# Earlier copies of second products, half of the taps' copies on VectorE, and an earlier last maximum, in a one-core convolution and mixture kernel

## The chip, the core and the metric

The kernel runs on one core of a Trainium2 chip. Its engines are TensorE (PE in the profile, its weight loads PEld), VectorE (DVE), ScalarE (ACT), GpSimd (POOL) and SyncE (SP), which only issues DMAs here. Each engine takes its own instructions in the order in which they are written, and waits for the others by semaphores. The metric is the device time of one execution in microseconds, the median of several runs; lower is better.

## The reference

The input is 8 sequences of 4160 positions with 192 numbers each. A causal convolution with 7 taps, softmax weights and 8 heads of 24 columns comes first; each of the 33280 rows then passes a layer with 1024 hidden columns:

```python
w = softmax(weight)                       # 8 heads x 7 taps
x = sum_k w[head, k] * x_pad[s + k]       # causal, per head
h = x @ w_in                              # 192 -> 1024
e = np.exp(h - h.max(-1))
solu = h * e / (e.sum(-1) + 1e-09)
ln = (solu - mean(solu)) / np.sqrt(var(solu) + 1e-06) * g_ln
out = ln @ w_out                          # 1024 -> 192
```

## The kernel before

The 33280 rows are 260 tiles of 128 rows. A tile i passes these stages, each a function that emits one or a few instructions:

- first products `ph` (PE): 128x1024 sums in one of three pairs of PSUM banks, from `yT` (the convolved rows, transposed) and the halves `whi`, `wlo` of `w_in`. The "thirds" are products of 64 rows each (line 794) that close a sum or open it.
- `emit_max` (DVE, L867): scales `ph` in place and finds the row's extreme. `emit_exp` (ACT, L874): exponentials `e` with their sum. `emit_mul` (DVE, L884): `e` times `ph`; it is the last reader of `ph`, so the pair of banks is free after it.
- `emit_hi` (ACT, L895, for some early tiles POOL, L893) and `emit_lo` (POOL, L910): the two halves `p` of `e` in 16 bits, and a transposing DMA `pT<-p`. `emit_square` (ACT, L899): sum of squares.
- `emit_out` (PE, L945, in the middle of the run L812): the second product `po` from `pT` and the halves `ohl` of `w_out`, some six tiles later, into one of two single PSUM banks. `emit_evac` (DVE, L986): the copy of `po` into `raw`, which frees that bank. Rows are scaled and stored later.

The two single banks are handed out in turn by `single`; other users of them are the convolution's products `pc` (L299) and, in four places, the taps. So a second product must wait for the copy of the second product before it whenever one other user stands between them.

The order on every engine is that of the emitting code. `three_steps(i)` emits three tiles a, b, c = i, i+1, i+2 and the second products of three earlier ones (`done`), for i = 8, 11, ... 29 and for i = 254; `two_steps` emits two tiles for 32 to 253; `leave_two` finishes the last pair; `last_three(257)` ends the program. Below, "step 17" is `three_steps(17)`, and "maximum of 17" is `emit_max` of tile 17.

`split_taps(q)` prepares the convolution's taps in 16 bits for the chunks from the fourth on. It runs four times: once at the last place of step 14 and at three places of step 17 (ahead of the first copy, inside `second()`, and ahead of the maximum of c). Each takes a single bank, `tph`, writes 448 columns with two matmuls (L611), and copies the high and low halves out on ACT (L617), 128x224 each.

In step 17 and step 20, `second()` (the second product of `done[1]` and the place of work after it) and the copy of `done[1]` stand after the multiplication of a. In `two_steps` the maximum of b is the last DVE work of the pair but one; the two copies of its pair of second products come at the start of the next pass or of `leave_two`.

Of the kernel before, what the change touches and what calls it, by code (L numbers as in the profile page):

```python
# [20 lines left out]
def kernel(  # L21
# [21 lines left out]
    NT = B * S // P  # L43
# [32 lines left out]
    act, dve, pool = nc.scalar, nc.vector, nc.gpsimd  # L76
# [499 lines left out]
    taps_hi = cp.tile([P, H, CW], F16, name="taps_hi")  # L576
# [5 lines left out]
    def of_blocks(t, a, z):  # L582
        return t[:, :, a * TB : z * TB].rearrange("p h (q c) -> p q h c", c=TB)
# [23 lines left out]
    def split_taps(q):  # L607

        t = single(f"tph_{q}")
        for j in range(2):  # L610
            nc.tensor.matmul(  # L611
                t[:, 2 * j * H * TB : 2 * (j + 1) * H * TB], spread(q + j),
                b16.rearrange("p a h c -> p (a h c)"), start=j == 0, stop=j == 1,
            )
        got = t[:, 0 : 4 * H * TB].rearrange("p (q a h c) -> p a q h c", q=2, a=2, h=H)
        for j, to in enumerate((taps_hi, taps_lo)):
            act.copy(of_blocks(to, q, q + 2), got[:, j])  # L617


    t_in = cp.tile([P, 1], F32, name="t_in")  # L620
# [243 lines left out]
    def emit_max(t):  # L864

        t.bias = sp.tile([P, 1], F32, name=f"sm_{t.i}", tag="sm", bufs=4)
        dve.tensor_scalar(  # L867
            t.ph, t.ph, t.cv[:, 0:1], None, ALU.mult, ALU.min, accum_out=t.bias
        )
# [12 lines left out]
    def emit_mul(t):  # L882

        dve.scalar_tensor_tensor(  # L884
            t.e, t.ph, t.cv[:, 3:4], t.e, ALU.mult, ALU.mult,
            accum_out=t.grp.s1[:, t.g : t.g + 1],
        )
# [92 lines left out]
    def emit_evac(t):  # L980
        if t.grp.raw is None:
            t.grp.open()
        if not t.wide:
            dve.tensor_copy(t.grp.raw[:, t.g, :], t.po[:, 0:D])
        else:
            dve.tensor_reduce(  # L986
                t.grp.raw[:, t.g, :],
                t.po[:, 0 : 2 * D].rearrange("p (a d) -> p d a", a=2), AX.X, ALU.add,
            )
        (rows if t.grp.ready else t.grp.waiting).append((t.grp, t.g))  # L990
# [432 lines left out]
    def three_steps(i):  # L1423
# [43 lines left out]
        def second():  # L1467
            for d in done[1:2]:
                emit_out(d)
            place(2)  # L1470
# [88 lines left out]
        if start:  # L1559
            if not behind:  # L1560
                root_squares()
            second()
            if i > PAIRED:
                if not behind:
                    for k, h in late:
                        sum_up(k, h, i - 1)
                    late.clear()
                uppers(2)
            for k, q in doubles:
                k.double(*q)  # L1570
            doubles.clear()
        emit_mul(a)
        if i == PAIRED:
            uppers(2)
# [17 lines left out]
        if start:  # L1592
            loads(work)
        else:
            second()
            uppers(2)
        for d in done[1:2]:
            emit_evac(d)
        run_chain(4)
        queue.run(3.8 if i < 20 else 2.0)  # L1600
        if start:
# [107 lines left out]
    def two_steps(i):  # L1709


        a, b = prepare(i), prepare(i + 1)
        x, z = tiles[i - 6], tiles[i - 5]
        ch, s = b.ch, b.k // 2
        c1, c3 = (chunks[ch + j] if ch + j < NCH else None for j in (1, 3))

        run_stores()
        first = ch == 3
        when = (2, 3, 5, 6) if first else (0, 1, 2, 4)
        if c3 and s in when:  # L1720
            c3.load(when.index(s))
        evacs = []
        if left_over:
            pa, pb, *evacs = left_over
            emit_exp(pb)
        else:
            pa = pb = None
        for d in evacs:
            emit_evac(d)
        if pb:  # L1730
            emit_mul(pb)

        got, summed = [], False
        sa, sb, sc = ring
        up_half(a, sa, 0)
        up_half(b, sb, 0)
        up_half(a, sa, 1)
        if s % 2 and c1:
            j = s - 1
            got, half, bank = fold(c1, c1.groups()[j : j + 2], sc)  # L1740
            out_half(x, z, 0, slice(0, 6))
            half(0)
            out_half(x, z, 0, slice(6, NFC))
            half(1)
            if chain and chain[0][1] is not None and chain[0][1] <= i + 2:
                add_up(i + 2, bank)
                summed = True
            ring[:] = [sa, sc, sb]
        else:
            out_half(x, z, 0)  # L1750
            ring[:] = [sc, sa, sb]
        up_half(b, sb, 1)
        out_half(x, z, 1)

        def move():
            for f in moves[:1]:
                f()
            del moves[:1]

        if pa:  # L1760
            emit_square(pa)
            emit_hi(pb)
            emit_lo(pa, pool)
        else:
            for q in squares:
                emit_square(q)
            squares.clear()
        for k, q in doubles:
            k.double(*q)
        doubles.clear()  # L1770
        move()
        emit_max(a)
        emit_exp(a)
        queue.run(1.3)
        for _ in range(2 + (len(rows) > 8)):
            if rows:
                g, j = rows.pop(0)
                g.row(j, act if j % 2 else dve)
        if not summed:
            run_chain(3)  # L1780
        if c3:
            for j in (
                ((), (), (), (0, 1), (2,), (3,), (4, 5), (6, 7)) if first
                else ((), (0,), (1,), (2,), (3,), (4,), (5, 6), (7,), ())
            )[s]:
                sum_up(c3, c3.halves(j // 2)[j % 2], i)
        for k, pc, hg in got[:1]:
            k.upper(pc, *hg)
        emit_mul(a)
        for k, pc, hg in got[1:]:  # L1790
            k.upper(pc, *hg)
        for k, pc, hg in got:
            k.lower(pc, *hg)
        if pb:
            emit_square(pb)
            emit_lo(pb, pool)
            queue.run(1.3)
        move()
        emit_hi(a)
        if summed:  # L1800
            run_chain(1)
        emit_max(b)
        run_chain(4)
        queue.run(1.3)
        if got and s in (3, 7):
            part = c1.parts[s == 7]
            if s == 3:
                c1.open(lefts[c1.ch], chunks[ch])
            moves.extend(
                lambda blk=blk: c1.turn(blk, *part) for blk in (1, 0, 2)  # L1810
            )
            moves.append(lambda: doubles.append((c1, part)))
        take_rooted()
        left_over[:] = [a, b, x, z]

    def leave_two():

        a, b, *done = left_over
        run_stores()
        emit_exp(b)  # L1820
        for d in done:
            emit_evac(d)
        emit_mul(b)
        emit_square(a)
        emit_hi(b)
        emit_lo(a, pool)
        emit_lo(b, pool)
        squares.append(b)

    def last_three(i):  # L1830


        a, b, c = [prepare(i + j) for j in range(3)]
        done = tiles[i - DEPTH : i]
        assert all(t.grp.n == 1 for t in (*done[4:], a, b, c))
        run_stores()
        take_rooted()
        emit_out(done[0])
        done = done[1:]
        emit_a(a, b, c, lambda: emit_out(done[0]), slots=tuple(ring))  # L1840
        for t in (b, c):
            emit_rows(t, False, True)
        for t in squares:
            emit_square(t)
        emit_evac(tiles[i - DEPTH])
        emit_evac(done[0])
        emit_max(a)
        emit_exp(a)
        emit_max(b)
        emit_exp(b)  # L1850
        emit_out(done[1])
        emit_mul(a)
        emit_halves(a, pool)
        emit_mul(b)
        emit_max(c)
        emit_out(done[2])
        emit_halves(b, pool)
        emit_exp(c)
        emit_evac(done[1])
        emit_evac(done[2])  # L1860
        emit_out(done[3])
        emit_mul(c)
        ready(done[4])
        emit_finish(done[3])
        emit_halves(c, dve)
        for t in (a, b, c):
            emit_square(t)
        emit_out(done[4])
        emit_finish(done[4])
        take_rooted()  # L1870
        queue.run(100.0)
        emit_out(a)
        ready(a)
        emit_finish(a)
        ready(b)
        ready(c)
        while rows or rooted:
            take_rooted()
            run_rows(i)
        run_stores()  # L1880
        for t in (b, c):
            emit_out(t)
            emit_finish(t)
        assert not stores and not queue.items
# [38 lines left out]
```

## Time and profile before

| | us |
|---|---|
| median of 3 runs (lowest, highest) | 1140.63 (1140.18, 1142.14) |
| profiled execution, its own time | 1142.65 |
| span in its profile | 1140.9 |
| PE busy | 1118.9 |
| ACT busy | 996.2 |
| DVE busy | 989.8 |
| POOL busy | 893.0 |

The span runs from the first to the last instruction; what lies around it (1.75 us) belongs to the execution's own time. Rows of a timeline give start, duration, engine, line, operation, output and inputs, partitions x elements, and in brackets how long the engine sat idle just before and who released it. The granted TensorE clock is 1.00 over the whole run.

### The profile page before, as it was taken

The page shows a single profiled execution, that of the slowest core. Times are in us where ns is not written, and L with a number is a line of the kernel's source. Part 1 is how long each engine was busy: PE and PEld are TensorE (multiplying, and loading weights), DVE is VectorE, ACT ScalarE, POOL GpSimd, SP SyncE. Part 2 cuts the span into 40 slices and gives each one's busy share as a digit, 9 for nine tenths or more (in the row PEclk, how much of TensorE's full clock was granted, in tenths as well). Part 3 has the DMA queues.
Part 4 walks back from the last instruction along what each step waited for, and adds up shares of the span by engine and source line. Part 5 has one row for each costly group of instructions (what it writes and reads, how often), then busy time and mean ns, then how long its engine had stood idle before and what let it go on. Part 6 is the DMA issues. An engine that isn't in the chain of part 4 may idle for free.

```text
span 1140.9 us, 34827 instructions
## 1 busy us (share of the span) xinstructions
PE 1118.9 (98%) x13693; PEld 912.7 (80%) x13693; DVE 989.8 (87%) x2024; ACT 996.2 (87%) x1789; POOL 893.0 (78%) x711
## 2 busy tenths in 40 slices
PE   6999999999999999999999999999999999999998
PEld 3675658878889988888888988888898888887866
DVE  7988898888898888889889888888988888878787
ACT  7888998888889888888888888898888889888895
POOL 2866899968889697888868879698787969855664
PEclk9999999999999999999999999999999999999999
DMA  7998999999999999999999999999999988779977
GB/s 220 197 188 181 218 216 195 198 216 213 225 211 204 225 190 207 206 200 208 208 191 202 195 212 218 178 208 209 210 212 204 216 185 156 183 155 212 184 151 180
DMA packets 727473, 227.75 MB, mean 200 GB/s; under 512 B 651646, under 2 KB 725902, under 8 KB 727310
## 3 DMA queue, kind: packets, MB, share of 16 engines
q1 hardware_dynamic: 727310, 225.53, 99.8%
q8 instruction: 108, 1.77, 0.7%
q14 instruction: 55, 0.45, 0.1%
HBM read 33.00 MB, written 25.56 MB: 51 GB/s over the span
## 4 chain that ended last, share of the span: by engine, by line
PE 70%; issue 9%; DVE 9%; ACT 6%; POOL 3%; DMA 2%; SPq 1%; DVEq 0%; ACTq 0%; POOLq 0%
PE ph L812 30%; PE po L812 28%; DVE ph L867 5%; PE pc L812 5%; PE po L945 3%; PE ph L765 2%; ACT e L874 2%; POOL p L910 2%; DVE e L884 1%; ACT sq L899 1%; DVE y L340 1%; PE pc L299 1%; DMA pT<-p 1%; DMA raw_in<-in_moe_w_in_dram 1%; PE ph L794 1%
## 5 line engine op out<-in xcount | busy, mean ns | idle before, releaser
L910 POOL TENSOR_TENSOR p<-e,p 128x1024 f16<-128x1024 f32 x257 | 548.5, 2137 | 113.0 <-ACT p L895 111.9
L812 PE MATMUL po<-ohl,pT 64*128 64x192 f16 (+1 forms) x5952 | 500.3, 283 | 1.2 <-DMA pT<-p 1.2
L812 PE MATMUL ph<-whi,yT 64*128 64x512 f16 x2664 | 487.6, 376 | 0.0
L812 PEld LDWEIGHTS <-pT 64*128 64x128 f16 x5952 | 401.5, 94 | 36.6 <-issue 4.2
L884 DVE SCALAR_TENSOR_TENSOR e<-ph,cv,e 128x1024 f32<-128x1024 f32 x248 | 318.0, 1283 | 115.4 <-ACT e L874 114.1
L812 PEld LDWEIGHTS <-yT 64*128 64x128 f16 x3774 | 288.6, 94 | 89.6 <-DMA yT<-y 0.5
L874 ACT ACTIVATE e<-ph,sm 128x1024 f32<-128x1024 f32 x260 | 289.6, 1114 | 78.2 <-DVE ph L867 67.2
L867 DVE TENSOR_SCALAR_CACHE_REDUCE ph<-ph,cv 128x1024 f32<-128x1024 f32 x248 | 318.7, 1287 | 1.8 <-PE ph L794 0.7
L812 PE MATMUL ph<-wlo,yT 64*128 64x512 f16 x1110 | 294.8, 376 | 0.0
L895 ACT CAST p<-e 128x1024 f16<-128x1024 f32 x245 | 255.8, 1045 | 41.8 <-DVE e L884 39.8
L899 ACT ACTIVATE sq<-e 128x1024 f32<-128x1024 f32 x260 | 273.3, 1051 | 0.2
L812 PE MATMUL po<-ohl,sixth 64*128 64x384 f16 (+1 forms) x1152 | 155.5, 283 | 0.0
L986 DVE TENSOR_REDUCE raw<-po 128x192 f32<-128x384 f32 x247 | 126.7, 550 | 1.8 <-PE po L945 1.7
L261 POOL TENSOR_TENSOR xs<-xr,xs 128x960 f16<-128x960 f32 (+1 forms) x56 | 107.7, 1924 | 0.8
L812 PEld LDWEIGHTS <-sixth 64*128 64x128 f16 x1152 | 102.6, 94 | 7.0 <-DMA sixth<-p 0.4
L812 PE MATMUL ph<-wlo,y 64*128 64x512 f16 x222 | 83.5, 376 | 0.3 <-DMA y<-yT 0.2
L945 PE MATMUL po<-ohl,pT 128*128 128x192 f16 (+1 forms) x696 | 78.2, 268 | 3.0 <-DVE raw L986 1.9
L945 PEld LDWEIGHTS <-pT 128*128 128x128 f16 x696 | 60.5, 98 | 21.7 <-issue 5.3
L812 PE MATMUL pc<-xs,taps_hi 64*112 64x240 f16 (+1 forms) x832 | 77.1, 258 | 0.2
L183 DVE TENSOR_REDUCE xa<-xr 128x1 f32<-128x384 f32 x112 | 67.6, 619 | 1.6 <-DMA xr<-in_x_dram 1.6
L340 DVE SCALAR_TENSOR_TENSOR y<-pc,y 112x432 f16<-112x432 f32 (+5 forms) x140 | 67.7, 531 | 1.1 <-ACT y L331 0.2
L812 PE MATMUL pc<-xs,taps_lo 64*112 64x240 f16 (+1 forms) x416 | 67.0, 258 | 0.0
(172 smaller groups left out, 1112.5 us busy)
## 6 DMA issues: line engine op xcount, KB each, us to landing
out_dram<-raw SPq DMA_DIRECT2D x127, 192.0 KB, 2.5
xr<-in_x_dram SPq DMA_DIRECT2D x41, 480.0 KB, 5.0
xr<-in_x_dram SPq DMA_DIRECT2D x22, 384.0 KB, 4.2
pT<-p SPq DMA_TRANSPOSE x226, 4.3
y<-yT SPq DMA_DIRECT2D x15, 140.0 KB, 3.4
y<-yT SPq DMA_DIRECT2D x15, 126.0 KB, 3.4
yT<-y SPq DMA_TRANSPOSE x102, 3.5
raw_out<-in_moe_w_out_dram SPq DMA_DIRECT2D x1, 1536.0 KB, 11.0
```

The costliest lines, as they stand in the source:

```text
L183: dve.tensor_reduce(self.part[:, col : col + 1], self.raw[j][:, a:z, :], AX.XY, ALU.max, apply_absolute_value=True,)
L261: (2.1 * size + 0.2, lambda: pool.tensor_tensor(xl, r, h, ALU.subtract)),
L340: dve.scalar_tensor_tensor(self.at(1, col + e, col + z, a, b), pc[:, :, e:z], self.scale(), self.at(0, col + e, col + z, a, b), ALU.mult, ...
L812: nc.tensor.matmul(o, lhs, w, start=start, stop=stop)
L867: dve.tensor_scalar(t.ph, t.ph, t.cv[:, 0:1], None, ALU.mult, ALU.min, accum_out=t.bias)
L874: act.activation(t.e, t.ph, AF.Exp, bias=t.bias, scale=-1.0, accum_out=grp.z[:, g : g + 1])
L884: dve.scalar_tensor_tensor(t.e, t.ph, t.cv[:, 3:4], t.e, ALU.mult, ALU.mult, accum_out=t.grp.s1[:, t.g : t.g + 1],)
L895: act.copy(t.p16[:, :, 0, :], t.halves)
L899: act.activation(junk, t.e, AF.Square, accum_out=t.grp.s2[:, t.g : t.g + 1])
L910: eng.tensor_tensor(t.p16[:, :, 1, :], t.halves, t.p16[:, :, 0, :], ALU.subtract)
L945: nc.tensor.matmul(t.po[:, 0:n], t.pT[:, a, :], w, start=j == 0, stop=j == len(ops) - 1)
L986: dve.tensor_reduce(t.grp.raw[:, t.g, :], t.po[:, 0 : 2 * D].rearrange("p (a d) -> p d a", a=2), AX.X, ALU.add,)
```

## The change

Four edits. `split_taps` copies the low half on DVE. Steps 17 and 20 emit `second()` and the copy of `done[1]` ahead of the multiplication of a. The last pass of `two_steps` leaves the maximum of its second tile to `leave_two`, which puts the two copies ahead of it. `last_three` puts maximum and exponentials of c, and the copy of `done[1]`, ahead of the multiplication of b.

```diff
@@ split_taps
-        for j, to in enumerate((taps_hi, taps_lo)):
-            act.copy(of_blocks(to, q, q + 2), got[:, j])
+        act.copy(of_blocks(taps_hi, q, q + 2), got[:, 0])
+        dve.tensor_copy(of_blocks(taps_lo, q, q + 2), got[:, 1])
@@ three_steps
             for k, q in doubles:
                 k.double(*q)
             doubles.clear()
+        elif i in (17, 20):
+            second()
+            for d in done[1:2]:
+                emit_evac(d)
         emit_mul(a)
...
         if start:
             loads(work)
         else:
-            second()
+            if i not in (17, 20):
+                second()
             uppers(2)
-        for d in done[1:2]:
-            emit_evac(d)
+        if i not in (17, 20):
+            for d in done[1:2]:
+                emit_evac(d)
@@ two_steps
-        emit_max(b)
+        if i < NT - 8:
+            emit_max(b)
@@ leave_two
         run_stores()
-        emit_exp(b)
         for d in done:
             emit_evac(d)
+        emit_max(b)
+        emit_exp(b)
         emit_mul(b)
@@ last_three
         emit_mul(a)
         emit_halves(a, pool)
+        emit_max(c)
+        emit_exp(c)
+        emit_out(done[2])
+        emit_evac(done[1])
         emit_mul(b)
-        emit_max(c)
-        emit_out(done[2])
         emit_halves(b, pool)
-        emit_exp(c)
-        emit_evac(done[1])
         emit_evac(done[2])
```

PE, POOL and SP keep their order; only DVE and ACT change theirs. The rows below are instructions of the built programs with the engines whose semaphores they wait for in brackets ("Activation" is ACT); a number in a name counts buffers.

On DVE at the end of step 14, after the multiplication of tile 15 (`e_1128`), stands the copy of the second product of tile 11 (`po_1195`), then the maximum of tile 16:

```order
 L884 SCALAR_TENSOR_TENSOR e_1128,s_8_696<-ph_1101,cv_429,e_1128 128x1024 [waits Pool_49]
-L986 TENSOR_REDUCE raw_1047<-po_1195 128x192 [waits PE_49]
+L617 CAST taps_lo<-tph_1212 128x2x8x14 [waits Activation_49]
+L986 TENSOR_REDUCE raw_1047<-po_1195 128x192
 L867 TENSOR_SCALAR ph_1102,sm_1218<-ph_1102,cvm_993 128x1024
```

The taps' copy now stands ahead of the copy of tile 11 and waits for ACT; the copy of tile 11, which waited for PE, has no wait of its own any more.

On DVE in step 17, from the maximum of 18 on (`e_1302` and `e_1306` belong to tiles 17 and 18, `ph_1282` to 19; `po_1322`, named `po_1310` after the change, and `po_1366` are the second products of 13 and 14):

```order
 L867 TENSOR_SCALAR ph_1281,sm_1304<-ph_1281,cv_760 128x1024 [waits PE_49]
-L884 SCALAR_TENSOR_TENSOR e_1302,s_16_1066<-ph_1250,cv_760,e_1302 128x1024 [waits Activation_49]
-L986 TENSOR_REDUCE raw_1047<-po_1322 128x192 [waits PE_49]
-L884 SCALAR_TENSOR_TENSOR e_1306,s_16_1066<-ph_1281,cv_760,e_1306 128x1024 [waits Activation_49]
-L867 TENSOR_SCALAR ph_1282,sm_1388<-ph_1282,cv_760 128x1024 [waits DVE_49,PE_49]
-L986 TENSOR_REDUCE raw_1047<-po_1366 128x192 [waits PE_49]
+L617 CAST taps_lo<-tph_1327 128x2x8x14 [waits Activation_49]
+L986 TENSOR_REDUCE raw_1047<-po_1310 128x192
+L884 SCALAR_TENSOR_TENSOR e_1302,s_16_1066<-ph_1250,cv_760,e_1302 128x1024 [waits Pool_49]
+L884 SCALAR_TENSOR_TENSOR e_1306,s_16_1066<-ph_1281,cv_760,e_1306 128x1024 [waits Pool_49]
+L617 CAST taps_lo<-tph_1383 128x2x8x14 [waits Activation_49]
+L867 TENSOR_SCALAR ph_1282,sm_1388<-ph_1282,cv_760 128x1024 [waits DVE_49]
```

Two taps' copies came in here, each with a wait for ACT, and the copy of tile 13 moved ahead of the multiplication of 17; the copy of 14 still follows the maximum of 19. The third, on `tph_1276`, stands some rows earlier in the same way: ahead of the copy of tile 12, which then precedes the maxima of 17 and 18. On ACT in the same step only the high halves are left, and the third of them moved ahead of the high half of tile 17 (`p_17`).

On DVE in `leave_two` (tile 252 is `e_19858`, tile 253 `ph_19753`; `po_19773` and `po_19774` are the second products of 246 and 247):

```order
 L884 SCALAR_TENSOR_TENSOR e_19858,s_252_19732<-ph_19742,cv_16474,e_19858 128x1024 [waits Activation_49]
-L867 TENSOR_SCALAR ph_19753,sm_19877<-ph_19753,cv_16474 128x1024 [waits PE_sequencer_49,DVE_49,PE_49]
 L986 TENSOR_REDUCE raw_19453<-po_19773 128x192 [waits PE_sequencer_49,PE_49]
 L986 TENSOR_REDUCE raw_19453<-po_19774 128x192
-L884 SCALAR_TENSOR_TENSOR e_19890,s_252_19732<-ph_19753,cv_16474,e_19890 128x1024 [waits Activation_49]
+L867 TENSOR_SCALAR ph_19753,sm_19890<-ph_19753,cv_16474 128x1024 [waits DVE_49]
+L884 SCALAR_TENSOR_TENSOR e_19892,s_252_19732<-ph_19753,cv_16474,e_19892 128x1024 [waits Activation_49]
```

The maximum of 253 moved behind the two copies, right ahead of its own multiplication. Step 254 then opens the first product of tile 256 in the pair of banks that tile 253 had; its first third waits for that multiplication.

## The prediction

> **What bounds the kernel now.** I read the page's busy times first, then what PE waited for, then PE, ACT and DVE row by row where the edits lie (99 to 126 us and from 1099 us on).
>
> ```profile
> span 1140.9 us, 34827 instructions
> PE 1118.9 (98%) x13693; PEld 912.7 (80%) x13693; DVE 989.8 (87%) x2024; ACT 996.2 (87%) x1789; POOL 893.0 (78%) x711
> PE po L945 <- DVE raw L986: 1.9, 3, 0.9
> L617 ACT CAST taps_lo<-tph 128x224 f16<-128x224 f32 x4 | 1.5, 370 | 0.0
> L984 DVE COPY raw<-po 128x192 f32<-128x192 f32 x8 | 2.7, 350 | 0.0
> ```
>
> PE is busy 98% of the span, so the end moves only by what is added to or taken from PE's 22 us of idle time. The change's own target is the third row: PE waited 3 times, 1.9 us in all, for a copy of a second product. Here is PE where that happens and around it (tiles 12 to 15 and 17; the first row is from the program's start):
>
> ```profile
> 10.27 1.94 PE L299 MATMUL pq<-xr,sixth 128*112 128x120 f32 x8 [2.08 <-ACT sixth L597]
> ...
> 101.48 2.12 PE L945 MATMUL po<-ohl,pT 128*128 128x384 f16 x16
> 106.21 2.13 PE L945 MATMUL po<-ohl,pT 128*128 128x384 f16 x16
> 111.20 2.12 PE L945 MATMUL po<-ohl,pT 128*128 128x384 f16 x16 [0.94 <-DVE raw L986]
> 115.07 2.12 PE L945 MATMUL po<-ohl,pT 128*128 128x384 f16 x16
> 125.15 2.12 PE L945 MATMUL po<-ohl,pT 128*128 128x384 f16 x16 [0.43 <-DVE raw L986]
> ```
>
> ACT in step 14's end and step 17 runs with no gap from row to row, and with its taps' copies late in its queue:
>
> ```profile
> 102.01 0.33 ACT L617 CAST taps_hi<-tph 128x224 f16<-128x224 f32 x1
> 102.48 1.13 ACT L874 ACTIVATE e<-ph,sm 128x1024 f32<-128x1024 f32 x1
> 107.31 0.34 ACT L617 CAST taps_hi<-tph 128x224 f16<-128x224 f32 x1
> 108.14 1.12 ACT L874 ACTIVATE e<-ph,sm 128x1024 f32<-128x1024 f32 x1
> 109.22 1.13 ACT L874 ACTIVATE e<-ph,sm 128x1024 f32<-128x1024 f32 x1
> 110.31 1.07 ACT L899 ACTIVATE sq<-e 128x1024 f32<-128x1024 f32 x1
> 111.35 1.06 ACT L895 CAST p<-e 128x1024 f16<-128x1024 f32 x1
> 112.76 1.14 ACT L252 ACTIVATE xs<-xr,s 128x960 f16<-128x960 f32 x1
> 113.76 1.08 ACT L899 ACTIVATE sq<-e 128x1024 f32<-128x1024 f32 x1
> 114.80 1.07 ACT L895 CAST p<-e 128x1024 f16<-128x1024 f32 x1
> 115.74 0.39 ACT L617 CAST taps_hi<-tph 128x224 f16<-128x224 f32 x1
> 116.21 1.17 ACT L874 ACTIVATE e<-ph,sm 128x1024 f32<-128x1024 f32 x1
> ```
>
> DVE in the same time: the copies (L986) of tiles 11, 12 and 14, maxima (L867) of 16 to 19, multiplications (L884) of 16 to 19:
>
> ```profile
> 100.30 0.55 DVE L986 TENSOR_REDUCE raw<-po 128x192 f32<-128x384 f32 x1
> 100.77 1.28 DVE L867 TENSOR_SCALAR_CACHE_REDUCE ph<-ph,cvm 128x1024 f32<-128x1024 f32 x1
> 103.73 1.28 DVE L884 SCALAR_TENSOR_TENSOR e<-ph,cvm,e 128x1024 f32<-128x1024 f32 x1 [0.50 <-ACT e L874]
> 105.60 0.55 DVE L986 TENSOR_REDUCE raw<-po 128x192 f32<-128x384 f32 x1
> 106.53 1.28 DVE L867 TENSOR_SCALAR_CACHE_REDUCE ph<-ph,cv 128x1024 f32<-128x1024 f32 x1
> 107.73 1.29 DVE L867 TENSOR_SCALAR_CACHE_REDUCE ph<-ph,cv 128x1024 f32<-128x1024 f32 x1
> 109.38 1.28 DVE L884 SCALAR_TENSOR_TENSOR e<-ph,cv,e 128x1024 f32<-128x1024 f32 x1 [0.31 <-ACT e L874]
> 111.06 1.28 DVE L884 SCALAR_TENSOR_TENSOR e<-ph,cv,e 128x1024 f32<-128x1024 f32 x1
> 112.26 1.29 DVE L867 TENSOR_SCALAR_CACHE_REDUCE ph<-ph,cv 128x1024 f32<-128x1024 f32 x1
> 113.46 0.56 DVE L986 TENSOR_REDUCE raw<-po 128x192 f32<-128x384 f32 x1
> 117.51 1.28 DVE L884 SCALAR_TENSOR_TENSOR e<-ph,cv,e 128x1024 f32<-128x1024 f32 x1 [2.04 <-ACT e L874]
> ```
>
> So DVE comes to each place of a taps' copy ahead of ACT: at 100.30 in step 14, where ACT reaches its high half at 102.01; at 105.60 in step 17, where ACT reaches it at 107.31. Before the change nothing tied the two.
>
> **The change, part by part.** *Taps' low halves on DVE, with the earlier copy in step 17.* The order rows decide this part. Each new copy on DVE waits for an ACT semaphore, and the copy of a second product behind it lost its own wait for PE. That fits only if the awaited ACT instruction itself follows PE's taps product, which stands behind that second product on PE. On ACT the high half of the same `tph` is the one that waits for it. So I take it that DVE's low half starts when ACT's high half has ended. The Trainium skill, "PSUM — Partial Sum Buffer", section "PSUM bank collisions raise a hardware error", says that two engines may not touch one PSUM bank at a time, two readers included, and that the hardware does not arbitrate, so software must order them; by that rule the wait is real and the sum is the one below, without it the sum is the rival's; the trace before shows no pair of readers, both halves being on ACT.
>
> The price of the copy itself: DVE's nearest row is a 128x192 copy of 0.35 us; the 128x384 sum of 0.55 us is the other bound. A DVE row is followed by the next some 0.08 us before its duration is over (100.30 to 100.77 for 0.55), so 0.27 to 0.47; for 224 columns I take 0.30. A semaphore costs about 0.05.
>
> Now I carry the times on, each from rows above; a maximum ends 1.34 us after its start (1.20 plus its 0.14 read-out).
>
> Step 14: DVE is free at 100.30 and waits for the high half's end at 102.34 (102.01 + 0.33). Its copy 102.38, tile 11's copy 102.68 to 103.23, so tile 12's second product starts at 103.29 and not at 101.48: PE +1.81. The maximum of 16 starts at 103.15 (before 100.77) and ends at 104.49, so exp of 16 on ACT goes from 102.48 to 104.59: +2.11 on ACT, and through it on the multiplication of 16.
>
> Step 17, first place: ACT, which has no gap to give, reaches its high half at 109.42 (107.31 + 2.11), end 109.76. DVE gets there at 107.71 (105.60 + 2.11) and stands until 109.80. Copy of taps, tile 12's copy 110.10 to 110.65, tile 13's second product at 110.71, before 106.21: PE +4.50, of which 2.69 is new. The maximum of 17 follows 0.93 after that copy's start, at 111.03; that of 18 at 112.23, end 113.57.
>
> Second place: exp of 17 at 112.42, exp of 18 at 113.67 (after its maximum), square 1.09 later, high half 1.04 later at 115.80, end 116.14. DVE, free at 113.43, waits to 116.18; taps; tile 13's copy, ahead of the multiplication now, 116.48 to 117.03; tile 14's product at 117.09, before 111.20: PE +5.89. The 0.94 of before is in this: 2.33 instead, so 1.39 is new. Here `second()` and its early copy bring nothing, because they stand behind a taps' copy that waits for a square.
>
> Third place: multiplications of 17 and 18 from 116.95 and 118.16 (the first ends at 118.24, the second leaves DVE free at 119.36). ACT: high half of 17 at 118.29; from there to the last taps copy 3.92 us (111.35 to 115.74, less 0.47 for the two taps' copies that stood at 112.29 and now are gone or ahead), 122.21, end 122.60. DVE waits from 119.36 to 122.64; taps; maximum of 19 at 122.94; tile 14's copy 1.20 later, 124.14 to 124.69; tile 15's product at 124.75, before 115.07: PE +9.68, of which 3.79 new.
>
> After that the multiplication of 19, which before waited 2.04 us for ACT, starts at about 126.1 (+8.6): DVE and ACT are late by less than PE and no longer hold it; POOL, whose low halves wait on ACT, is late by less still. With 98% busy PE gives none of the 9.68 back.
>
> *Earlier copy in step 20.* No taps stand there; tile 16's copy moves ahead of a 1.27 us multiplication, and the 0.43 wait at 125.15 goes: -0.43. The multiplication of 20 starts 0.47 later; ACT's high half takes it into ACT's relative slack of about 1 us.
>
> *Maximum of 253 behind the copies.* The rows at the end (DVE, then PE, then SP's transposes for the last tiles):
>
> ```profile
> 1100.29 1.29 DVE L867 TENSOR_SCALAR_CACHE_REDUCE ph<-ph,cv 128x1024 f32<-128x1024 f32 x1
> 1101.49 1.02 DVE L986 TENSOR_REDUCE raw<-po 128x192 f32<-128x384 f32 x2
> 1102.97 1.28 DVE L884 SCALAR_TENSOR_TENSOR e<-ph,cv,e 128x1024 f32<-128x1024 f32 x1 [0.46 <-ACT e L874]
> 1102.10 2.12 PE L945 MATMUL po<-ohl,pT 128*128 128x384 f16 x16 [0.54 <-DVE raw L986]
> 1104.60 0.38 PE L794 MATMUL ph<-wlo,yT 64*128 64x512 f16 x1
> 1125.15 5.93 SPq L927 DMA_TRANSPOSE pT<-p x4
> ```
>
> The copies can start at 1100.29, so PE's wait of 0.54 goes. But maximum, exp and multiplication of 253 come 0.94 later (two copies of 0.47): the multiplication, 1102.97 to 1104.26 before, ends at 1105.20. The third at 1104.60 opens tile 256's sum in the banks of 253 and waits for it: it starts at 1105.25, +0.65 against before, though PE would have been there at 1104.06. Net +0.65.
>
> *Last three tiles.* The multiplication of 259 comes some 0.4 us earlier, but the last transposes stand in SP's queue behind four others that run back to back from 1125.15, released by the multiplication of 257, which does not move: 0. That of 258 starts about 1.5 us later, within SP's spacing.
>
> Sum: 1.81 + 2.69 + 1.39 + 3.79 - 0.43 + 0.65 = +9.90 us. On the profiled execution's own 1142.65 that gives 1152.55; that execution ran 2.02 us above the median, and on the median of 1140.63 it gives **1150.5**.
>
> **Rivals.** *DVE does not wait* (the other side): the ACT instruction it waits for is an older one, already done. Then ACT is 4 x 0.23 us freer and DVE 4 x 0.30 fuller: the stalls of 0.94, 0.43 and 0.54 go, at most -1.9, and the four copies of 0.30 and the 0.65 + 0.54 at 1104.60 come, at most +2.4. It gives 1138.7 to 1143.0, about 1141. It decides if the high half has ended before DVE arrives: by 100.30 in step 14, where the row says 102.34. Against it speaks the lost wait for PE.
>
> *The clock falls.* PE would stand still for up to 3.79 us at a stretch, longer than the 2.08 us of the row at 10.27, after which the clock was still 1.00. If it halved for as long as the longest stall lasted, half of that would be lost: +1.9, 1152.4. The Trainium skill, "TensorE: Matmul & The Clock Gate", Part 1, puts the clock at half after an idle window of about 3.4 us and until a busy one of the same length; by its figures the estimate is 1.7 us for one such window, and no run here shows it in mid-kernel.
>
> *Stalls do not chain*: if ACT took back the 2.11 us before step 17's places, only the largest single wait (3.8) and the end would stay: 1140.63 + 3.8 + 0.2 = 1144.6. The ACT rows, back to back, speak against it.
>
> **How the numbers follow.** Forecast 0.78, clock 0.08, unchained stalls 0.05, no wait 0.09. What a measurement of this kernel can tell from no change is about 0.2%, 2.3 us; the no-wait case lies almost all within it. So faster 0.02, same 0.07, slower 0.91. The range: DVE's copy at 0.27 or 0.47 moves the sum by -0.1 to +0.7, four semaphore gaps by 0.4 either way, the third at 1104.60 by -1.2 if it doesn't wait, the clock by +1.9; a low end of 1147.0 also leaves room for part of the stalls to be taken back, the high end is 1153.5. Only the no-wait and the unchained case lie outside.
>
> **What would show it.** Right: PE's waits for `raw` (L986) grow from 1.9 us to about 11, in four gaps of about 1.8, 2.7, 2.3 and 3.8 us between 100 and 126 us, none at tile 17's product; DVE's idle time has a new releaser, ACT `taps_hi`, with about 2.0, 2.1, 2.7 and 3.3 us; and a PE wait for DVE `e` (L884) of about 1.1 us shows near 1114. Wrong: `taps_lo` on DVE starts without idle time, or PE's gaps stay under 1 us.

## The result, and the profile after

The changed kernel takes 1154.35 us (median of 6 runs, 1152.26 to 1157.98), the kernel before 1140.85 us beside it (6 runs, 1139.77 to 1142.14): a ratio of 1.0121 with a 95% interval of 1.0102 to 1.0141. It is slower, as forecast, but by 13.5 us and not by 9.9, and 0.85 us above the range. The profiled execution took 1157.98 us, the slowest of the six, so its rows are read term by term and not by its total.

The page's span and its busy times:

```profile
span 1156.3 us, 34828 instructions
PE 1124.3 (97%) x13693; PEld 918.9 (79%) x13693; DVE 991.3 (86%) x2028; ACT 995.4 (86%) x1785; POOL 891.9 (77%) x711
```

The span is 15.4 us longer than before's. PE's busy time grew by 5.4 us with the same 13693 matmuls, so its idle time grew by 10.0 us. These are two losses, longer waits and slower matmuls, and the forecast's sum has only the first. What PE waited for (us in all, times, longest):

```profile
PE po L945 <- DVE raw L986: 8.9, 4, 3.5
PE ph L794 <- DVE e L884: 1.1, 1, 1.1
PE pc L299 <- DVE y L340: 0.6, 2, 0.5
```

And the new entry among DVE's waits:

```profile
DVE taps_lo L617 <- ACT taps_hi L616: 9.7, 4, 3.1
```

The second products of tiles 11 to 17 on PE, to be held against the rows of before:

```profile
100.01 2.12 PE L945 MATMUL po<-ohl,pT 128*128 128x384 f16 x16
105.78 2.12 PE L945 MATMUL po<-ohl,pT 128*128 128x384 f16 x16 [1.73 <-DVE raw L986]
113.19 3.45 PE L945 MATMUL po<-ohl,pT 128*128 128x384 f16 x16 [2.62 <-DVE raw L986]
119.57 2.12 PE L945 MATMUL po<-ohl,pT 128*128 128x384 f16 x16 [1.01 <-DVE raw L986]
127.16 4.00 PE L945 MATMUL po<-ohl,pT 128*128 128x384 f16 x16 [3.55 <-DVE raw L986]
135.15 2.13 PE L945 MATMUL po<-ohl,pT 128*128 128x384 f16 x16
139.47 2.12 PE L945 MATMUL po<-ohl,pT 128*128 128x384 f16 x16
```

The products of tiles 13 and 15 take 3.45 and 4.00 us where all others take 2.12. The stretches around them say why (length, busy time of each engine, then the granted clock, the DMA share and GB/s):

```profile
34.00:38.00 4.00, 4.00 (x21) 4.00 (x22) 2.60 (x7) 4.00 (x7) 4.00 (x3) 0.57 0.58 113
112.00:118.00 6.00, 4.81 (x25) 2.90 (x26) 3.78 (x7) 3.66 (x7) 5.25 (x4) 0.72 0.31 70
127.00:135.00 8.00, 7.84 (x36) 4.50 (x36) 3.88 (x9) 5.77 (x10) 7.50 (x6) 0.62 1.12 209
```

The clock was 1.00 in all three in before. It fell to one half inside the second stall (at 112.52 us) and inside the fourth (at 126.18 us), and once at 34 us, in the start of the program, where the change does nothing. Below, a fall "after" a stall is one of this kind: its slow matmuls come when the stall ends. That first fall, and some 0.7 us by which the start was slower before it, make tile 11's second product 2.41 us late (100.01 against 97.60); everything below is counted from there.

### The profile page after: what moved, and what is told of

Its sections match the earlier page's. It is cut to its first block, busy times and chain, and to the rows that moved or that the text cites. A ratio compares the mean times of both kernels' runs of the same rounds, so it can differ in the third digit from the quotient of the medians.

```text
span 1156.3 us, 34828 instructions
## 1 busy us (share of the span) xinstructions
PE 1124.3 (97%) x13693; PEld 918.9 (79%) x13693; DVE 991.3 (86%) x2028; ACT 995.4 (86%) x1785; POOL 891.9 (77%) x711
## 4 chain that ended last, share of the span: by engine, by line
PE 62%; DVE 13%; issue 13%; ACT 8%; DMA 2%; POOL 1%; SPq 0%; DVEq 0%; ACTq 0%; POOLq 0%
PE ph L812 26%; PE po L812 23%; DVE ph L867 8%; PE pc L812 4%; PE po L945 3%; PE ph L765 3%; ACT e L874 3%; DVE e L884 2%; ACT sq L899 2%; DVE y L340 1%; PE pc L299 1%; DMA xr<-in_x_dram 1%; ACT p L895 1%; ACT y L331 1%; DMA raw_in<-in_moe_w_in_dram 1%
## 5 line engine op out<-in xcount | busy, mean ns | idle before, releaser
L895 ACT CAST p<-e 128x1024 f16<-128x1024 f32 x245 | 255.8, 1045 | 44.1 <-DVE e L884 42.8
L945 PE MATMUL po<-ohl,pT 128*128 128x192 f16 (+1 forms) x696 | 81.4, 274 | 9.3 <-DVE raw L986 8.9
L340 DVE SCALAR_TENSOR_TENSOR y<-pc,y 112x432 f16<-112x432 f32 (+5 forms) x140 | 67.7, 531 | 2.1 <-ACT y L331 1.3
```

Source lines behind the costliest of these rows:

```text
L340: dve.scalar_tensor_tensor(self.at(1, col + e, col + z, a, b), pc[:, :, e:z], self.scale(), self.at(0, col + e, col + z, a, b), ALU.mult, ...
L895: act.copy(t.p16[:, :, 0, :], t.halves)
L945: nc.tensor.matmul(t.po[:, 0:n], t.pT[:, a, :], w, start=j == 0, stop=j == len(ops) - 1)
```

## The experiments

To compare profiles with different starts I use one number: the start of the n-th exponentials on ACT (line 874, 260 in each kernel) less the same in before, less that difference at tile 11. The last column is that difference at tile 11, the lateness of the start. The ratios are not the quotients of the medians given beside them; a loss in us that follows a ratio is worked out from it.

| kernel | tile 16 | 17 | 19 | 20 | 30 | start |
|---|---|---|---|---|---|---|
| changed | 2.11 | 4.32 | 8.09 | 11.98 | 12.55 | 2.40 |
| e9, the same again | 2.10 | 4.31 | 8.08 | 10.55 | 11.12 | 2.26 |
| e10, PE filled | 2.11 | 4.32 | 8.09 | 9.13 | 9.70 | 0.68 |
| e8, late copy in step 17 | 2.11 | 4.32 | 6.38 | 7.43 | 8.00 | 0.18 |
| e2, taps alone | 2.10 | 4.31 | 6.37 | 7.42 | 7.72 | 0.17 |
| e7, last place alone | 0.01 | 0.01 | 1.70 | 2.74 | 3.04 | -0.07 |
| e6, first place alone | 2.11 | 2.12 | 2.12 | 2.11 | 2.10 | 0.17 |
| e1, taps back on ACT | 0.00 | 0.00 | 0.00 | 0.00 | 0.20 | 1.24 |
| e3, low half first | 0.02 | 0.13 | -0.20 | -0.26 | 0.19 | 0.60 |

**Taps back on ACT (e1).**

```diff
-        act.copy(of_blocks(taps_hi, q, q + 2), got[:, 0])
-        dve.tensor_copy(of_blocks(taps_lo, q, q + 2), got[:, 1])
+        for j, to in enumerate((taps_hi, taps_lo)):
+            act.copy(of_blocks(to, q, q + 2), got[:, j])
```

> The changed kernel with both halves of the taps copied on ACT again, so that only the three reorderings are left. Theory A (the whole loss is VectorE waiting for ACT's high half, and what follows from it): no PE wait for raw between 100 and 126 us but the one of the second product after step 14, the clock at 1.00 from 40 us to the end, and 0.94 + 0.43 + 0.54 us of waits gone against 1.1 us that come at the last pair: 1139.5 to 1141. Theory B (the reorderings cost a good part of the 13 us): 1144 or more. Theory C (the half clock at 34 to 37 us comes with the changed program): a half-clock stretch there in this kernel too, about +1.7 us.

Measured: 1141.92 us against 1141.0, ratio 1.0007 (0.9998 to 1.0017). The 13 us are gone, so they come from the copies of the taps; theory B falls. But the reorderings bring nothing either, where A had up to 1.5 us: the median lies above A's range. PE's rows of e1 show where step 17's 0.94 us and step 20's 0.43 us went:

```profile
111.34 2.12 PE L945 MATMUL po<-ohl,pT 128*128 128x384 f16 x16
117.66 0.26 PE L299 MATMUL pc<-xs,taps_hi 128*112 128x240 f16 x1 [0.32 <-ACT taps_lo L617]
118.57 0.26 PE L299 MATMUL pc<-xs,taps_hi 128*112 128x240 f16 x1 [0.64 <-POOL xs L261]
128.56 0.36 PE L299 MATMUL pc<-xs,taps_hi 128*112 128x240 f16 x2 [0.47 <-DVE y L340]
```

Tile 14's product no longer waits, and 6 us later the convolution's product waits 0.96 us for its inputs. In step 20 the copy that was moved ahead delays the multiplication behind it by 0.47 us, and the loss comes back to PE by way of ACT:

```profile
126.30 1.04 ACT L895 CAST p<-e 128x1024 f16<-128x1024 f32 x1 [0.35 <-DVE e L884]
127.25 0.56 ACT L331 ACTIVATE y<-pc 112x480 f16<-112x480 f32 x1
127.85 0.66 DVE L340 SCALAR_TENSOR_TENSOR y<-pc,y 112x480 f16<-112x480 f32 x1 [0.38 <-ACT y L331]
```

ACT's high half (L895) waits 0.35 us for that multiplication, ACT's part of the convolution's `y` (L331) stands behind it, DVE's part (L340) waits 0.38 us for ACT's, and the next convolution product waits 0.47 us for that. In before no row in these places shows a wait. Of theory C: e1 has the half clock at 34 us too, but so have e4, e9 and e11, and e2, e3, e5 to e8 and e10 have not. e11 is the same program as before up to the last pair of tiles. So it is a matter of the run, not of the change.

**Taps alone (e2)**: the kernel before with the `split_taps` part of the change and nothing else.

> The kernel before with the low halves on VectorE and nothing else changed. Theory A: four VectorE waits for ACT's taps_hi of 2.0 to 3.1 us, PE waits for raw of 8 to 11 us in all, and a half clock after each PE gap of over 2.2 us: 1152 to 1156, as the whole change. Theory B: under 1147.

Measured: 1150.59 us, ratio 1.0081 (1.0066 to 1.0097), that is +9.2 us. The mechanism is there (four DVE waits for `taps_hi`, 7.8 us in all), but the median lies between the ranges of the two theories. Without the earlier copy in step 17 the last stall is 0.90 us and not 3.55, so PE waits 7.5 us for `raw` in all where A had 8 to 11, and only one half clock follows, at 110.85 us.

**Low half first (e3).** The two lines of `split_taps` change places:

```diff
-        act.copy(of_blocks(taps_hi, q, q + 2), got[:, 0])
         dve.tensor_copy(of_blocks(taps_lo, q, q + 2), got[:, 1])
+        act.copy(of_blocks(taps_hi, q, q + 2), got[:, 0])
```

> The changed kernel with the two copies of split_taps emitted in the other order: VectorE's low half first, ACT's high half second. If two readers of one bank are put in order, ACT is now the one that waits, and comes 1.7 us after VectorE anyway. Theory A: VectorE waits for ACT nowhere at taps_lo, PE's waits for raw under 1 us in all, clock 1.00 after 40 us, 1139.5 to 1141. Rival (the four added VectorE copies of 0.39 us cost PE by themselves, or VectorE now waits for PE's taps product as long): 1143 or more.

Measured: 1142.76 us, ratio 1.0013 (1.0004 to 1.0022), between the ranges of theory A and the rival. DVE's four copies, first to last:

```profile
100.90 0.38 DVE L616 CAST taps_lo<-tph 128x224 f16<-128x224 f32 x1
106.21 0.38 DVE L616 CAST taps_lo<-tph 128x224 f16<-128x224 f32 x1
109.84 0.39 DVE L616 CAST taps_lo<-tph 128x224 f16<-128x224 f32 x1
113.44 0.39 DVE L616 CAST taps_lo<-tph 128x224 f16<-128x224 f32 x1 [0.34 <-PE tph L611]
```

The same instructions on the same engines, in the other order, and 12 of the 13 us are gone: DVE waits 0.34 us, for PE, instead of 9.7 us for ACT. This is the experiment that names the cause: the order of the two readers. Whether it is the bank or the tile `tph` that ties them no run separates, as both halves always lie in one tile in one bank. What is left over 1141 fits the two edits at the end (+1.7 us alone, in e11): at tile 30 the table has 0.19 us for e3.

**Both halves on DVE (e4)**: `dve.tensor_copy` for both.

> The changed kernel with both halves copied on VectorE, so that there is no second engine on the taps' bank at all, and VectorE waits for PE alone. Theory A: 1139.5 to 1141.5, eight copies of 0.39 us on VectorE hidden beside PE, ACT 1.9 us less busy. Rival (VectorE's added time reaches PE): four times 0.6 us more, 1142.5 to 1143.5.

Measured: 1143.73 us, ratio 1.0023 (1.0012 to 1.0034). No wait for ACT is left, but the doubled copies do reach PE: 1.7 us of waits for `raw` in two places. Theory A's range is missed; the rival had the better size.

**PE filled in its gaps (e5, e10).** Matmuls of whi by whi are written into banks whose reader is done, or zeros are added to a sum that is still open, just ahead of the four second products that wait.

```diff
+            if i == 17:
+                fill(tiles[15].ph, 4)
+            if i == 20:
+                fill(tiles[18].ph, 12)
             if swap:
                 emit_out(done[0])
...
+            if a.i == 17 and t is c and n == 0:
+                fill(c.ph, 8)
             emit_third(t, n, low, t is c or (t is b and not last))
...
+        if i == 17:
+            fill(c.ph, 6, True)
         emit_rows(c, False, True)
```

> The changed kernel with 30 added matmuls of 512 columns, whose results are thrown away or are zeros, in the four places where PE stands still: 4, 8, 6 and 12 of them (0.215 us each) ahead of the second products of tiles 12 to 15. The waits themselves stay. Theory A (the half clock that follows the long gaps is the part which the forecast lacked): clock 1.00 from 100 to 140 us, second products of 2.12 us everywhere, the four products start at the times that the stalls alone give (+9.7 us at tile 15), 1150 to 1152. Theory B (what is over the forecast is a longer wait, and the clock costs nothing beside it): 1153.5 to 1155, as the changed kernel.

e5 measured 1153.29 us (ratio 1.0104, 1.0087 to 1.0121), which lies between the two theories' ranges, and against other runs of before than the 1154.35. So both kernels ran again side by side.

> The changed kernel once more, beside the filled one, so that the two stand against the same runs of before. Theory A (half clock): 1153.5 to 1155.5, at least one half-clock stretch between 105 and 135 us, and 2 to 3 us above the filled kernel. Theory B (the clock costs nothing beside the waits): within 1 us of the filled kernel.

> The changed kernel with the 30 filling matmuls once more. In its first profile tile 20's exponentials stood 9.1 us later than in before, against 12.0 in the changed kernel, but the two medians (1153.3, 1154.35) came from different calls. Theory A: 1151 to 1152.5, 2 to 3 us under the changed kernel of this call. Theory B: 1153.5 to 1155, within 1 us of it.

Measured: the changed kernel 1154.95 us (ratio 1.0115, 1.0099 to 1.0130), the filled one 1153.91 us (1.0109, 1.0095 to 1.0122). The medians are 1.04 us apart, which is theory B's forecast rather than A's 2 to 3, and the intervals overlap. The clock over whole runs speaks for A: its mean was 0.996 or less in all ten runs of the changed kernel and 0.997 or more in all eight of the filled one, and the changed kernel's four runs at 0.996 took 1152.26 to 1153.83 us, its six at 0.993 to 0.995 took 1154.73 to 1157.98 us. The mean does not say where in a run the clock fell, and the start can have a fall too. The profiles do tell the theories apart in the stretch in question. The filled kernel's second products of tiles 11 to 16 (its lines stand 15 lower):

```profile
98.29 2.12 PE L960 MATMUL po<-ohl,pT 128*128 128x384 f16 x16
104.06 2.12 PE L960 MATMUL po<-ohl,pT 128*128 128x384 f16 x16 [0.87 <-DVE raw L1001]
111.47 2.12 PE L960 MATMUL po<-ohl,pT 128*128 128x384 f16 x16 [0.68 <-DVE raw L1001]
117.85 2.12 PE L960 MATMUL po<-ohl,pT 128*128 128x384 f16 x16 [1.05 <-DVE raw L1001]
125.44 2.12 PE L960 MATMUL po<-ohl,pT 128*128 128x384 f16 x16 [0.96 <-DVE raw L1001]
130.59 2.13 PE L960 MATMUL po<-ohl,pT 128*128 128x384 f16 x16
```

and its clock in the same two stretches, then e9's:

```profile
112.00:118.00 6.00, 4.95 (x31) 2.78 (x29) 3.40 (x7) 3.68 (x7) 3.61 (x3) 1.00 0.24 54
127.00:135.00 8.00, 8.00 (x56) 4.72 (x55) 6.60 (x11) 6.35 (x12) 7.07 (x5) 1.00 1.14 205
```

```profile
112.00:118.00 6.00, 4.96 (x24) 3.06 (x25) 3.78 (x7) 3.65 (x8) 5.15 (x3) 0.72 0.30 65
127.00:135.00 8.00, 7.99 (x48) 4.69 (x49) 5.26 (x11) 5.60 (x11) 7.50 (x5) 0.81 1.14 208
```

With the gaps filled the clock stays at 1.00 in both profiled runs, every product takes 2.12 us, and tile 15's starts 9.68 us late (125.44 less 115.07, less 0.69 for the start). e5's profile gives the same (9.14 at tile 20, 9.71 at tile 30). In the table the fall after the second stall costs nothing (8.09 at tile 19 with and without it): the slower product only uses up part of the stall that comes next. The fall after the fourth stall has no stall behind it and is paid in full, 1.42 us in e9 (10.55 less 9.13, half clock for 3.41 us) and 2.85 us in the first profile (11.98 less 9.13, for 6.82 us). Why do the medians show only 1.04 us of it? The profiles give one reason: both filled ones lose 1.2 us in the last stores, which SP issues in 3.2 us where all others need 1.97 to 1.99. The filled kernel first, then e9:

```profile
1144.89 3.20 SPq L1081 DMA_DIRECT2D out_dram<-raw  x4
```

```profile
1148.62 1.98 SPq L1066 DMA_DIRECT2D out_dram<-raw  x4
```

What makes those stores slow there was not settled, nor whether they are slow in the runs that were not profiled.

**First place alone (e6)** and **last place alone (e7)**: the kernel before, with the low half on DVE for one of the four calls.

```diff
+            copy = dve.tensor_copy if j and q == 0 else act.copy   # e7: q == 6
+            copy(of_blocks(to, q, q + 2), got[:, j])
```

> The kernel before with the low half on VectorE at the first of the four places alone (end of step 14). Theory A (a PE stall is lost for good): one PE wait of 1.7 us ahead of tile 12's product, its start 1.8 us later, and the same 1.8 us still there at tile 17; 1142.5 to 1143.5. Rival (what PE loses there is taken back by waits that then end sooner, as the gain of 0.94 us was given back in the kernel with the taps back on ACT): 1141 to 1142.

> The kernel before with the low half on VectorE at the last of the four places alone. By the rows of before VectorE is free at 113.5 us, ACT's high half ends at 116.1, the maximum (1.20) and the copy (0.55) follow, so tile 15's product starts at 118.2 and not at 115.07: one stall of about 3.1 us with no stall ahead of it. Theory A (a gap of this length is followed by a half clock): 3.1 us and 1.4 to 2.9 more, 1145.5 to 1147. Theory B (no half clock, or it costs nothing): 1144 to 1144.5. Rival (stalls do not add up, since one place costs as much as four): 1150 or more.

e6 measured 1144.66 us against 1141.54, ratio 1.0017 (0.9999 to 1.0035), that is +1.9 us. The median lies above both forecast ranges, the loss is theory A's 1.8. Its interval just holds no change; the table is clearer: 2.11 us at tile 16 are still 2.10 at tile 30, and 1.80 at tile 258 (both profiles lose some 2 us near 230 us, see the last section, so they can be compared that far). In this profile the loss on PE stays. e7 measured 1144.29 us, ratio 1.0029 (1.0018 to 1.0040), that is +3.3 us. One row of its profile:

```profile
118.30 2.12 PE L946 MATMUL po<-ohl,pT 128*128 128x384 f16 x16 [3.13 <-DVE raw L987]
```

The stall is the 3.1 us worked out, and here no half clock followed: the product takes 2.12 us. So theory B holds for this profile. e7's ten runs spread from 1143.19 us at a mean clock of 1.000 to 1147.96 us at 0.996, and its six runs at 0.999 or more took 1143.19 to 1144.30 us, the four at 0.998 or less 1145.15 to 1147.96. That fits a fall in some runs only; where it fell is not known, as their traces were not taken.

**Late copy in step 17 (e8)**: the changed kernel with `elif i == 20:` for `elif i in (17, 20):`, and the other two conditions to match.

> The changed kernel with step 17's second product of tile 13 and its copy put back behind the multiplication of tile 17 (step 20 stays changed). Theory A (ahead of the multiplication they put the wait for a square in front of it, and so make the last place's wait longer): the stall ahead of tile 15 falls from 3.55 to about 1 us, no half clock after it, 1150 to 1152. Theory B (the place of this copy doesn't matter, as the forecast had it): 1153.5 to 1155.

Measured: 1150.25 us, ratio 1.0080 (1.0061 to 1.0100), in theory A's range. That is 4.1 us less than the changed kernel's 1154.35, which was taken beside other runs of before (by the ratios it is 4.7). The two programs differ in the earlier copy in step 17 alone, whose target was the wait of 0.94 us. DVE's rows in e8:

```profile
113.88 1.28 DVE L884 SCALAR_TENSOR_TENSOR e<-ph,cv,e 128x1024 f32<-128x1024 f32 x1
117.30 0.39 DVE L617 CAST taps_lo<-tph 128x224 f16<-128x224 f32 x1 [2.13 <-ACT taps_hi L616]
118.07 1.28 DVE L884 SCALAR_TENSOR_TENSOR e<-ph,cv,e 128x1024 f32<-128x1024 f32 x1
121.03 0.39 DVE L617 CAST taps_lo<-tph 128x224 f16<-128x224 f32 x1 [1.67 <-ACT taps_hi L616]
```

With the multiplication of 17 ahead of the third taps' copy, ACT gets its work while DVE stands, and the last wait is 1.67 us. In the changed kernel that multiplication stands behind the wait, ACT then waits for DVE, and the last wait is 3.12 us. The stall that this last wait makes is longer (3.55 against 0.90 us; in the table 8.09 against 6.38 at tile 19). In e8 no half clock follows it: only the one at 111.26 us is left, in the second stall.

**The end alone (e11)**: the kernel before with the parts of the change in `two_steps`, `leave_two` and `last_three`.

> The kernel before with the two edits at the end alone: the maximum of tile 253 behind the two copies, and the order of the last three tiles. The forecast had +0.65 for the first and 0 for the second. The rows of the experiments so far say more: exponentials of tile 256 0.94 us later than those of tile 252, and 1.1 to 1.3 us at the end. Theory A (both cost): +1.0 to +1.3 us, a PE wait of 1.1 us for e near 1104, and the last PE wait (0.8 us for pT) gone without an earlier end. Forecast's sizes: +0.65. Rival (the end hides both): 0.

Measured: 1142.96 us against 1141.53, ratio 1.0015 (1.0005 to 1.0025), +1.7 us. In its profile, allowing for 0.22 us that it is late at 1098 us, tile 256's third starts 0.66 us late (1105.48 against 1104.60), waiting for the multiplication of 253:

```profile
1105.48 0.37 PE L794 MATMUL ph<-wlo,yT 64*128 64x512 f16 x1 [1.21 <-DVE e L884]
1129.19 0.91 DVE L997 TENSOR_TENSOR t<-z 128x1 f32<-128x1 f32 x1
```

The end of the span is 0.98 us late, so the last three tiles cost another 0.3 us. The second row is in that place: an operation on 128x1 elements that takes 0.90 or 0.91 us in all nine profiles with these edits and 0.16 us in the five without. In all nine it runs beside the last of POOL's products (L926) and ends 0.01 to 0.02 us after it; in the five POOL's product is over before it starts. That fits a wait for POOL, and 0.75 us would be what it adds; no run tried it. The last PE wait, which theory A had gone, is still 0.77 us, now for DVE (L998).

**A version to beat both (e12)**: the kernel before, `split_taps` as in e3, the earlier copy in step 17 only, and 11 matmuls that add zeros to the sums of tiles 2 and 3.

> A version meant to beat both: the kernel before, with the low half first on VectorE and the high half behind it on ACT, step 17's copy of tile 13 ahead of the multiplication, steps 20 and the end as before, and 11 matmuls that add zeros to the sums of tiles 2 and 3 in the two PE gaps at 27 and 31 us, after which three profiles had a half clock at 34 us (tile 11's exponentials 1.2 to 2.8 us late). Theory A: no half clock before 100 us in any run, 0.3 us less from step 17: a median of 1139.8 to 1140.8 against 1141, and fewer slow runs among its own. Rival (the added matmuls or the copies cost what they bring): 1141 to 1142.

Measured: 1141.36 us against 1141.53, ratio 1.0000 (0.9991 to 1.0009). It beats the changed kernel by 13 us and does not beat the one before: theory A's 1139.8 to 1140.8 is missed, and the rival's range holds. Its profile has no half clock before the end, and step 17 gains 0.27 us until tile 20, of which 0.08 us is left at tile 24; neither shows in the median.

## Why the forecast's direction was right and its size wrong

Term by term, from tile 11's product on (the last two from e11, whose edits they are):

| step of the forecast | forecast | measured |
|---|---|---|
| step 14 | +1.81 | +1.89 |
| step 17, first place | +2.69 | +2.68 |
| step 17, second place | +1.39 | +1.39 |
| step 17, third place | +3.79 | +3.72 |
| half clock after the fourth stall | 0 | +1.42 (e9), +2.85 |
| earlier copy in step 20 | -0.43 | 0 |
| maximum of 253 | +0.65 | +0.66 |
| last three tiles | 0 | +0.3 |
| sum | +9.90 | +12.1 to +13.5 |

- *The wait of DVE's low half for ACT's high half* was right: DVE's four idle times were forecast as 2.0, 2.1, 2.7 and 3.3 us and are 1.99, 2.01, 2.60 and 3.12. e3 shows that it is the order of two readers of one tile in one bank. This is what the section "PSUM bank collisions raise a hardware error" of the Trainium skill ("PSUM — Partial Sum Buffer") makes software do; the runs show the wait, not what would happen without it. The rival without a wait fell.
- *The chain* was right to 0.1 us at each place; the changed kernel and the filled one both have tile 15's product 9.68 us late, which is the forecast's number. The rival of unchained stalls fell with it, and in e6's profile PE gives next to nothing back (1.80 of 2.11 us are left at tile 258).
- *The clock* is the step that failed. It stood as a rival with a chance of 0.08 and +1.9 us, so the sum had it at nothing; the runs show it as a term of 1.42 to 2.85 us. The forecast took a gap of 2.08 us without a fall (at 10.27 us) to mean that 3.79 us was needed to be in doubt, though the fall after the third place's stall then has nothing behind it to hide it. A gap of 2.62 us was followed by a half clock in the changed kernel, e2, e8 and e9, one of 3.55 us in the changed kernel and e9; the one of 3.13 us in e7's profile was not, so the term has a chance and no sharp limit. Near in it was the price: 1.42 us for 3.41 us of half clock, 2.85 for 6.82, on both sides of the forecast's 1.9 and of the 1.7 us estimated there from the Trainium skill ("TensorE: Matmul & The Clock Gate", Part 1).
- *The second place* started when forecast (5.96 us late in the changed and in the filled kernel, 5.89 forecast), because DVE's copy sets that start, but the wait ahead of it was 1.01 and not 2.33 us: the product ahead of it ran 1.33 us longer at half clock, inside the time that PE would have waited. That is also why PE's waits for `raw` add up to 8.9 us and not to the forecast's 11.
- *Step 20* was mis-sized: the 0.43 us go (tile 17's product has no wait), and the convolution's next product waits 0.47 us for `y`. What failed there is the 0.47 us that ACT's high half was to take into a slack of about 1 us: ACT stood idle 0.35 us for the multiplication, in the changed kernel too, and the convolution's `y` (L331) stands right behind that high half on ACT. I had followed the moved copy to the high half and not to the instruction behind it.
- *The end*: the first part as forecast, the second 0.3 us more.
- *The range* reached to 1153.5 with the clock's +1.9 as its largest single part. The misses on step 20 (0.43) and the end (0.3) add to that and were in no part of it; the runs of before stood 0.2 us higher as well. From their 1140.85 us the two sums give 1152.9 and 1154.3 us; the median, 1154.35, lies at the upper one, with the half clock of 6.82 us.

## What to carry to other kernels

When a copy out of a bank is split between two engines, as here, the second reader in program order can wait for the first: put the one whose engine arrives first in front, and count what is queued behind the other. A gain on one wait is only a gain if the next operand of the same engine is ready sooner too; look for the next two inputs, not one. A stall that ends with nothing idle behind it costs its length and, on PE, possibly a stretch at half clock after it. Here gaps of 2.62 and 3.55 us had one in every profile in which PE stood idle for them, the one of 3.13 us had none, and one of 1.73 us in the program's start had one in some profiles: price it as a term with a chance.

## What the runs showed of the hardware that I had not expected

The half clock comes and goes on a grid. In e9 it fell at 20.73, 34.39, 112.89 and 126.55 us and rose 3.41 us after each; the distances, 13.66, 78.50 and 13.66 us, are 4, 23 and 4 times 3.413 us. The Trainium skill says so too ("TensorE: Matmul & The Clock Gate", Part 1): a free-running window of 3.41 us. Where it differs: it puts the fall after an idle window, and here a window with PE at work for about half of it was enough. In e1 the clock fell at 33.97 us, right behind a window with 1.68 us of PE work; in e9 a window of the grid with 1.69 us of it, at the first stall, had no fall behind it:

```profile
30.56:33.97 3.41, 1.68 (x14) 1.25 (x13) 3.17 (x7) 3.41 (x6) 3.33 (x3) 1.00 1.27 219
```

```profile
102.65:106.07 3.42, 1.69 (x10) 0.73 (x9) 1.44 (x3) 1.92 (x5) 3.34 (x3) 1.00 0.61 138
```

So the busy time in the window does not decide by itself, and what else does stays open. The gap in e1's window is the 1.73 us before line 299 that all these kernels but e12 have, and 5 of 13 profiles of kernels with that gap had a fall before 40 us. Where the grid lies against the gap would make such a difference from run to run; no run could set it. In the other direction 2.43 us of work in a window at half clock were not enough to rise (the first profile, 126.18 to 129.59 us), and 2.94 were (e9).

The other thing that moves runs of one kernel is a transposing DMA. In before's own profile it holds PE at 228 us:

```profile
228.19 1.56 PE L812 MATMUL po<-ohl,pT 64*128 64x384 f16 x22 [1.20 <-DMA pT<-p]
```

Around it exponentials are 2.1 us later than in e1, e4 or e7, where PE doesn't wait there; e6's profile has a like loss, in two waits of 0.73 and 0.67 us. The size is near the 2.02 us by which before's execution stood above its median, but the runs at the median were not profiled.
